# Loading half of one section of w_mod in four-partition transfers, one per iteration, in a decode block on one Trainium2 core

## The chip, the cores and the metric

The kernel runs on one core of a Trainium2 chip. The metric is the device time of one launch in microseconds, as the median of several runs. A core has a matrix engine (TensorE, PE in the profile, with PEld for its weight loads), VectorE (DVE), ScalarE (ACT), GpSimd (POOL) and SyncE (SP), which here only issues transfers. Sixteen DMA engines move the data of all transfers between HBM and SBUF, which has 128 partitions.

## The reference

Four sequences, one new token each, go through one conditioned block: attention over a cache of 4096 positions with 32 heads, and a gated MLP. A modulation matrix w_mod (512 x 3072) turns the condition c into six sections of 512 columns: shift, scale and gate of the attention (sa, ca, ga) and of the MLP (sb, cb, gb).

```python
mod = (silu(c) @ w_mod).reshape(4, 6, 1, 512)
sa, ca, ga, sb, cb, gb = (mod[:, k] for k in range(6))
h = layernorm(x) * (1 + ca) + sa
q = (h @ wq)                                  # 32 heads of 128
p = softmax(q . k_cache * 128 ** -0.5)        # 4096 positions
x = x + ga * ((p @ v_cache) @ wo)
h = layernorm(x) * (1 + cb) + sb
z = gelu(h @ w_in)                            # 512 -> 2 x 896
g = w_sp * layernorm(z[896:]) + b_sp
x = x + gb * ((z[:896] * g) @ w_out)
```

Matrices and caches are bfloat16. The two caches have 134 MB each; everything else together has some 14 MB.

## The kernel before

The work is cut into NT = 32 tiles of 4 heads of one sequence: tile i has group g = i // 4 and sequence b = i % 4. A tile's K and its V are 4 MB each, 32 KB in every partition. Both have two buffers (`kt` and `vt`).

**Before the loop.** SyncE issues wq_sb, wm_sb (five of the six sections of w_mod, `wm[:, :, 0:5 * D]`, four rows of w_mod in each partition), K0, K1 and V0. ScalarE issues c_sb and x_sb, four partitions each. c is turned into columns by TensorE transposes (`rows_to_cols`, L184) and its silu is taken there on 128 x 16 elements (L225 to L234), which gives cT. `mod_cols` (L236) multiplies sections of wm_sb by cT, so that the result stands in columns. With the first two sections the kernel makes hT, and from that the queries qbc.

**The loop, L530.** The order on each engine is written out by hand (`manual_schedule`). In iteration i VectorE multiplies the two halves of K by the queries (`mult`, L288), TensorE adds up over the head dimension by products with the identity (`reduce_d`, L294), VectorE finishes the scores of tile i - 1 (`scores`), ScalarE takes the exponentials (L326), and TensorE multiplies V of tile i - 2 (`pv`, L366). After the second half of the reduction SyncE is told to load K of tile i + 2 (`load_k`), and after `pv` it loads V of tile i (`load_v`). SyncE has one queue and issues in program order; each K or V load waits until its buffer is free.

At i == 2 the next three sections of wm_sb (ga, sb, cb) are multiplied into `modT`, the pool `pre` that holds wq_sb and wm_sb is closed, and the pool `wts` takes its memory: wo_sb in four pieces and wo_last are loaded. At i == 5 one is added to the cb part of modT. At i == L - 1 = 30 come V31 in five pieces, win_sb, wout_sb, and the last section gb of w_mod into a V buffer (`wg_sb`, L602).

**The tail, from L604.** The last V pieces are multiplied as they land (`o_last`), the second layernorm gives hT2 (it needs the sb and cb parts of modT), `gate` (L684) multiplies it by win_sb, L707 multiplies by wout_sb, and L715 by the last section of w_mod. Then the row is written out.

Of the kernel before, what the change touches and what calls it, by code (L numbers as in the profile page):

```python
# [8 lines left out]
BF16 = mybir.dt.bfloat16  # L9
F32 = mybir.dt.float32  # L10
AF = mybir.ActivationFunctionType
ALU = mybir.AluOpType
# [12 lines left out]
def kernel(  # L25
# [16 lines left out]
    nc = tc.nc  # L42
    P = 128
    B, _, D = A_x.shape
    _, H, SK, DH = A_k_cache.shape
    F = B_w_in.shape[1]
    FH = F // 2
    DJ = D // P
# [10 lines left out]
    LN_EPS = 1e-5  # L59
    L = NT - 1  # L60
    BL = B - 1

    ctx.enter_context(tc.manual_schedule())

    consts = ctx.enter_context(tc.tile_pool(name="consts", bufs=1))
# [7 lines left out]
    def ps_sm(shape, dtype=F32):  # L73
        return psum.tile(shape, dtype, name="sm", bufs=3)
# [6 lines left out]
    pre = pre_cm.__enter__()  # L81
    c_sb = pre.tile([B, D], BF16, name="c_sb")
# [4 lines left out]

    wq_sb = pre.tile([P, DJ, H * DH], BF16, name="wq_sb")
    nc.sync.dma_start(out=wq_sb, in_=A_wq.rearrange("(p j) n -> p j n", p=P))
    wm_sb = pre.tile([P, DJ, 5 * D], BF16, name="wm_sb")  # L90
    wm = w_mod.rearrange("(p j) n -> p j n", p=P)
    nc.sync.dma_start(out=wm_sb, in_=wm[:, :, 0:5 * D])

    def kv_view(cache, i):
        g, b = divmod(i, B)
# [16 lines left out]
    def load_v(i):  # L112
# [8 lines left out]
    ident_bf = consts.tile([P, P], BF16, name="ident_bf")  # L121
    make_identity(nc, ident_bf)
    ident_f = consts.tile([P, P], F32, name="ident_f")
# [19 lines left out]
        out=sel32, in_=ident_f.rearrange("p (q r) -> p r q", r=R), axis=AX.X, op=ALU.add  # L143
# [10 lines left out]
    for g in range(G):  # L154
        nc.vector.tensor_reduce(out=selg[:, g:g + 1], in_=idr[:, g], axis=AX.XY, op=ALU.add)
    nc.vector.tensor_reduce(
        out=sel4, in_=ident_f.rearrange("p (c b) -> p b c", b=B), axis=AX.X, op=ALU.add
# [3 lines left out]
        out=mask8, in_=ident_f.rearrange("p (h u) -> p h u", h=2 * HQ), axis=AX.X, op=ALU.add  # L161
# [3 lines left out]
    x1w = consts.tile([P, DJ, R], F32, name="x1w")  # L165
    nc.gpsimd.memset(x1w, 0.0)
    cT = consts.tile([P, DJ, B], BF16, name="cT")

    consts.tile([P, 512], mybir.dt.uint8, name="gap")
    wk.tile([P, 32], mybir.dt.uint8, name="gap", bufs=1)  # L170
    pbds, opss = [], []
    for k in range(3):
        t = consts.tile([P, NJ, HQ], BF16, name=f"pbd{k}")
        nc.gpsimd.memset(t, 0.0)
        pbds.append(t)
    for k in range(2):
        t = psum.tile([P, G, DH], F32, name=f"ops{k}", bufs=1)
# [3 lines left out]
    def bc(ap, n):  # L181
        return ap[:, None, :].to_broadcast([P, n, ap.shape[-1]])

    def rows_to_cols(src):  # L184
        t = ps_sm([P, DJ, B], BF16)
        for j in range(DJ):
            nc.tensor.transpose(t[:, j, :], src[0:B, j:D:DJ], ident_bf[0:B, 0:B])
        return t

    def across(rhs, mat):  # L190
# [13 lines left out]
    def normed(pool, src, name, then=None, last=None):  # L204
# [16 lines left out]
        rsqrt(rs, v, 1.0, eps)  # L221
        return xc, rs

    cps = rows_to_cols(c_sb)
    cx = pre.tile([P, DJ, B], F32, name="cx")  # L225
    nc.vector.tensor_copy(out=cx, in_=cps)
    sg = pre.tile([P, DJ, B], F32, name="sg")
    nc.vector.tensor_scalar(
        out=sg, in0=cx, scalar1=-60.0, scalar2=-1.0, op0=ALU.max, op1=ALU.mult
    )  # L230
    nc.scalar.activation(out=sg, in_=sg, func=AF.Exp)
    nc.vector.tensor_scalar_add(out=sg, in0=sg, scalar1=1.0)
    nc.vector.reciprocal(out=sg, in_=sg)
    nc.vector.tensor_tensor(out=cT, in0=cx, in1=sg, op=ALU.mult)  # L234

    def mod_cols(s0, n, dst):  # L236

        for m in range(n):
            s, j = divmod(m, DJ)
            c0 = (s0 + s) * D + j  # L240
            for k in range(DJ):
                nc.tensor.matmul(  # L242
                    dst[:, m, :], lhsT=wm_sb[:, k, c0:c0 + (P - 1) * DJ + 1:DJ], rhs=cT[:, k, :],
                    start=(k == 0), stop=(k == DJ - 1),
                )
# [11 lines left out]
        out=hs, in0=modA[:, DJ:2 * DJ, :], scalar=1.0, in1=xn, op0=ALU.add, op1=ALU.mult  # L257
# [83 lines left out]
    def whole(i):  # L341

        g, b = divmod(i, B)
        return slice(b, b + 1) if g == NQ - 1 else slice(0, B) if b == BL else None

# [86 lines left out]
    for n in set(SETS):  # L432
        picks[n] = consts.tile([P, n, P], BF16, name=f"pick{n}")
        for a in range(n):
            u = P // n
            nc.vector.tensor_copy(
                out=picks[n][:, :, a * u:(a + 1) * u],
                in_=ident_bf.rearrange("p (u r) -> p r u", r=n),
# [79 lines left out]
    modT = consts.tile([P, 3 * DJ, B], F32, name="modT")  # L518
# [6 lines left out]
    def add_up():  # L525
        while adds:
            o_add(*adds.pop(0))

    QPLAN = {0: (1, 2), 1: (3, 4, 5), 2: (6, 7)}
    for i in range(NT):  # L530
        more = list(QPLAN.get(i, ()))
        mult(i, 0)
        if i >= 1:
            scores(i - 1)
        if i >= 2:
            norm_b(i - 2)
        add_up()
        rows_up()
        dealt()
        if i >= 3:  # L540
            o_pick(i - 3)
        reduce_d(i, 0)
        if i >= 3:
            o_cols(i - 3)
        if more:
            queries(more.pop(0))
        mult(i, 1)
        if i >= 1:
            norm_r(i - 1)
        if i >= 3:  # L550
            o_scale(i - 3)
        sum8(i, 0)
        reduce_d(i, 1)
        load_k(i + 2)
        if i >= 1:
            norm_a(i - 1)
        project()
        if i - 3 in ends:
            deal(ends[i - 3])
        while more:  # L560
            queries(more.pop(0))
        if i >= 2:
            pv(i - 2)
        if i == 0:
            load_v(1)
        elif 2 <= i < L:
            load_v(i)
        if i == 2:
            nc.scalar.dma_start(out=sp_t[:, 0:1], in_=B_w_sp[0:1, 0:1])
            nc.scalar.dma_start(out=sp_t[:, 1:2], in_=B_b_sp.rearrange("(a b) -> a b", b=1))  # L570
            mps = ps_sm([P, 3 * DJ, B])
            mod_cols(2, 3 * DJ, mps)
            nc.vector.tensor_copy(out=modT, in_=mps)
            pre_cm.__exit__(None, None, None)
            wts = tl = ctx.enter_context(tc.tile_pool(name="wts", bufs=1))
            wo_sb = wts.tile([P, H - HQ, D], BF16, name="wo_sb")
            wo_last = wts.tile([P, HQ, D], BF16, name="wo_last")
            hl = (H - HQ) * DH
            h0 = 0
            for n in SETS:  # L580
                nc.sync.dma_start(
                    out=wo_sb[:, h0:h0 + n, :],
                    in_=A_wo[h0 * DH:(h0 + n) * DH].rearrange("(p r) n -> p r n", p=P),
                )
                h0 += n
            nc.sync.dma_start(out=wo_last, in_=A_wo[hl:H * DH].rearrange("(q p) n -> p q n", p=P))
        if i == 5:
            sps = ps_sm([P, 2])
            nc.tensor.matmul(sps, lhsT=ones_b, rhs=sp_t, start=True, stop=True)
            nc.vector.tensor_copy(out=spf, in_=sps)  # L590
            nc.vector.tensor_copy(out=g8[:, 1, :], in_=spf[:, 0:1].to_broadcast([P, B]))
            cbT = modT[:, 2 * DJ:3 * DJ, :]
            nc.vector.tensor_scalar_add(out=cbT, in0=cbT, scalar1=1.0)
        if i == L - 1:
            load_v(L)
            win_sb = wts.tile([P, DJ, F], BF16, name="win_sb")
            nc.sync.dma_start(out=win_sb, in_=B_w_in.rearrange("(p j) n -> p j n", p=P))
            wout_sb = wts.tile([P, NH, D], BF16, name="wout_sb")
            nc.sync.dma_start(out=wout_sb, in_=B_w_out.rearrange("(j p) n -> p j n", p=P))
            wg_sb = kvp.tile([P, NJ, DH], BF16, name="vt", bufs=2)  # L600
            wg_sb = wg_sb.rearrange("p n d -> p (n d)")[:, 0:DJ * D].rearrange("p (k n) -> p k n", k=DJ)
            nc.sync.dma_start(out=wg_sb, in_=wm[:, :, 5 * D:])  # L602
# [17 lines left out]
    o_scale(L - 1)  # L620
    adds.append((o_proj(0, BL), 0, BL))
    add_up()
# [6 lines left out]
    def sums():  # L629
# [21 lines left out]
        out=nv2, in0=mq2[:, 0:1], scalar=mq2[:, 0:1], in1=mq2[:, 1:2],  # L651
        op0=ALU.mult, op1=ALU.subtract,
# [6 lines left out]
        out=hl, in0=xs, scalar=mq2[:, 0:1], in1=cbT[:, :, BL], op0=ALU.subtract, op1=ALU.mult  # L659
    )  # L660
    nc.vector.scalar_tensor_tensor(
        out=hT2[:, :, BL], in0=hl, scalar=rsl, in1=sbT[:, :, BL], op0=ALU.mult, op1=ALU.add
# [4 lines left out]
        out=x1m, in0=x1[:, :, :, None].to_broadcast([P, DJ, B, HQ]),  # L667
        in1=mask4[:, None, None, :].to_broadcast([P, DJ, B, HQ]), op=ALU.mult,
    )
    x1r = ps_sm([B * DJ, P])  # L670
    for k in range(DJ):
        nc.tensor.matmul(
            x1r[:, k:P:DJ], lhsT=x1m[:, k].rearrange("p b j -> p (b j)"), rhs=sel32,
            start=True, stop=True,
# [4 lines left out]
    def gate(h):  # L679
# [21 lines left out]
        out=zz.rearrange("p f g b -> p g b f"), in0=z1[:, None].to_broadcast([P, 2, B, NH]),  # L701
        in1=st3[:, 0:2], op=ALU.mult,
    )
    y = ps_q()[:, 0:DJ * 2 * B].rearrange("p (j g b) -> p j g b", j=DJ, g=2)
    for j in range(DJ):
        for f in range(NH):
            nc.tensor.matmul(  # L707
                y[:, j], lhsT=wout_sb[:, f, j * P:(j + 1) * P], rhs=zz[:, f],
                start=(f == 0), stop=(f == NH - 1),
# [3 lines left out]
    for j in range(DJ):  # L713
        for k in range(DJ):
            nc.tensor.matmul(  # L715
                gb[:, j, :], lhsT=wg_sb[:, k, j * P:(j + 1) * P], rhs=cT[:, k, :],
                start=(k == 0), stop=(k == DJ - 1),
# [3 lines left out]
        out=mq3, in_=ps3.rearrange("p (g b f) -> p g b f", g=2, b=B), axis=AX.X, op=ALU.add  # L721
# [4 lines left out]
        out=rs3, in0=mq3[:, 1], scalar=LN_EPS, in1=rs3, op0=ALU.add, op1=ALU.subtract  # L726
# [3 lines left out]
        out=g8[:, 0, :], in0=mq3[:, 0, :], scalar=-1.0, in1=g8[:, 1, :], op0=ALU.mult, op1=ALU.mult  # L730
# [5 lines left out]
        out=t3[:, 2], in0=yb[:, 0], scalar1=spf[:, 1:2], scalar2=None, op0=ALU.mult  # L736
    )
    nc.vector.tensor_tensor(
        out=g8, in0=g8, in1=rs3[:, None, :].to_broadcast([P, 2, B]), op=ALU.mult
    )  # L740
    nc.vector.tensor_tensor(
        out=t3[:, 0:2], in0=g8[:, :, :, None].to_broadcast([P, 2, B, DJ]), in1=yb, op=ALU.mult
# [3 lines left out]
        out=tt, in_=t3.rearrange("p g b j -> p b j g"), axis=AX.X, op=ALU.add  # L746
# [37 lines left out]
```

## Time and profile before

| what | value |
|---|---|
| time, median of 3 runs | 667.55 us (667.23 to 667.95) |
| span of the profiled execution, first to last instruction | 665.8 us |
| PE, DVE, ACT busy | 60%, 63%, 13% of the span |
| DMA | 283.15 MB, 425 GB/s, SyncE's queue 98.9% of 16 engines' span |
| K and V loads (4096 KB), issue to landing, median | 23.0 and 30.7 us |
| mean granted TensorE clock | 0.828 |

The time of the profiled execution itself is not listed apart from its span; the median of the runs is 1.75 us above that span. The profile's page gives the busy time of each engine, the span in 40 equal slices with a digit for the busy tenths, the DMA queues with packets, megabytes and their share of the DMA engines' time, the chain of waits that ended last, and the transfers with the time from their issue to landing. In the timeline a row has start and duration in us, engine and line, the tiles, and in brackets how long the engine had been idle and what ended that. A q behind an engine's name is its instruction queue, where transfers are issued.

### The profile page before, as it was taken

The numbers are of one execution on the slowest core, as the hardware profiler recorded it, in microseconds if no ns is written. First come the engines' busy times: TensorE is split into PE (matmuls) and PEld (weight loads), VectorE is DVE, ScalarE is ACT, GpSimd is POOL, SyncE is SP. The second block draws the span as 40 slices with busy tenths as digits, with TensorE's granted clock in tenths as the row PEclk, the third lists the DMA queues.
The fourth block names the chain that finished last, engine by engine and source line by source line (L and its number), as shares of the span: only waits on it lengthen the run. The fifth ranks groups of instructions, "written<-read, shape, count | busy, mean of one in ns | idle before, by whom it ended". The sixth has DMA issues, their size and how long they took to land.

```text
span 665.8 us, 6509 instructions
## 1 busy us (share of the span) xinstructions
PE 399.3 (60%) x2674; PEld 175.4 (26%) x2674; DVE 419.5 (63%) x589; ACT 85.0 (13%) x278; POOL 3.8 (1%) x17
## 2 busy tenths in 40 slices
PE   1195795556556746754665467566555468666675
PEld 0132331222222312222222222222222223322245
DVE  3485592776565777655567756657765566776833
ACT  1021120111011111101111110111111011111112
POOL 1000000000000000000000000000000000000000
PEclk9998987777898778789877778787777897887975
DMA  8999999999999999999999999999999999999996
GB/s 363 452 419 433 431 417 435 436 437 422 439 432 438 422 439 433 436 423 436 435 431 426 438 435 432 426 436 437 431 426 437 435 429 432 433 436 421 438 419 234
DMA packets 13377, 283.15 MB, mean 425 GB/s; under 512 B 1308, under 2 KB 3236, under 8 KB 4132
## 3 DMA queue, kind: packets, MB, share of 16 engines
q1 hardware_dynamic: 13328, 282.73, 98.9%
q8 instruction: 21, 0.34, 0.2%
q14 instruction: 8, 0.07, 0.0%
q10 hardware_dynamic: 20, 0.01, 0.0%
HBM read 282.73 MB, written 0.00 MB: 425 GB/s over the span
## 4 chain that ended last, share of the span: by engine, by line
DMA 56%; DVE 28%; PE 13%; issue 1%; SPq 1%; ACT 0%; DVEq 0%
DMA kt<-in_A_k_cache_dram 52%; DVE kt L288 21%; PE red L294 11%; DMA win_sb<-in_B_w_in_dram 5%; DVE osb L378 2%; DVE S L303 1%; DVE mrow L312 1%; DVE osb L374 1%; PE ops L366 1%; SPq L104 1%; DVE mt L316 1%; DVE nM L318 0%; PE qps L274 0%; DVE mb L314 0%; DVE nM L319 0%
## 5 line engine op out<-in xcount | busy, mean ns | idle before, releaser
L294 PE MATMUL red<-kt,ident_bf 128*128 128x512 bf16 x1024 | 301.5, 461 | 236.4 <-DVE kt L288 236.4
L288 DVE TENSOR_TENSOR kt<-kt,qbc 128x8192 bf16<-128x8192 bf16 x64 | 282.8, 4420 | 185.2 <-DMA kt<-in_A_k_cache_dram 184.2
L294 PEld LDWEIGHTS <-ident_bf 128*128 128x128 bf16 x1024 | 118.9, 116 | 411.5 <-issue 285.8
L326 ACT ACTIVATE pbd<-S,nM 32x128 bf16<-32x128 f32 x128 | 73.8, 577 | 505.3 <-DVE nM L319 463.2
L366 PE MATMUL ops<-vt,pbd 128*16 128x512 bf16 x992 | 62.6, 388 | 1.4 <-DMA vt<-in_A_v_cache_dram 1.4
L303 DVE TENSOR_REDUCE S<-red 128x64 f32<-128x512 f32 x64 | 43.8, 684 | 5.8 <-PE red L294 5.8
L378 DVE SCALAR_TENSOR_TENSOR osb<-ops,selg,osb 128x128 f32<-128x128 f32 x93 | 32.6, 351 | 3.3
L326 ACT ACTIVATION_READ_ACCUMULATOR pbd<-S,nM 32x1 f32 x128 | 32.0, 250 | 0.0
L366 PEld LDWEIGHTS <-pbd 128*16 128x16 bf16 x992 | 23.2, 90 | 30.7 <-issue 8.5
L386 PEld LDWEIGHTS sm<-sel,osb 128*128 128x128 f32 x62 | 11.7, 194 | 7.4 <-issue 2.2
L374 DVE TENSOR_SCALAR osb<-ops,selg 128x128 f32<-128x128 f32 x31 | 10.1, 325 | 5.3 <-PE ops L366 5.3
L386 PE MATMUL sm<-sel,osb 128*128 128x4 f32 x62 | 9.2, 219 | 2.1 <-DVE osb L378 2.0
L278 ACT CAST qbc<-qps 128x512 bf16<-128x512 f32 x8 | 4.7, 585 | 45.3 <-PE qps L274 45.3
L274 PE MATMUL qps<-wq_sb,hTb 128*32 128x512 bf16 x128 | 9.2, 412 | 1.6 <-DVE hTb L262 0.9
L312 DVE TENSOR_REDUCE mrow<-S 128x1 f32<-128x128 f32 x32 | 9.2, 286 | 1.1
L242 PE MATMUL sm<-cT,wm_sb 128*128 128x4 bf16 x80 | 3.0, 173 | 8.3 <-DMA wm_sb<-in_w_mod_dram 8.3
L316 DVE STREAM_TRANSPOSE mt<-mb 128x32 f32<-128x32 f32 x32 | 6.8, 212 | 1.1
L337 DVE TENSOR_SCALAR rsb<-mask,rs 128x4 f32<-128x4 f32 x32 | 7.2, 224 | 0.4 <-ACT pbd L326 0.4
L318 DVE TENSOR_REDUCE nM<-mt 128x1 f32<-128x32 f32 x32 | 6.0, 186 | 1.1
L314 DVE COPY mb<-mrow 128x32 f32<-128x32 f32 x32 | 5.8, 181 | 1.1
L491 PE MATMUL sm<-wo_sb,od 128*4 128x512 bf16 x24 | 5.7, 379 | 0.0
L319 DVE TENSOR_SCALAR nM<-nM 128x1 f32<-128x1 f32 x32 | 4.9, 153 | 1.1
(136 smaller groups left out, 88.8 us busy)
## 6 DMA issues: line engine op xcount, KB each, us to landing
kt<-in_A_k_cache_dram SPq DMA_DIRECT2D x31, 4096.0 KB, 23.0
vt<-in_A_v_cache_dram SPq DMA_DIRECT2D x31, 4096.0 KB, 30.7
wq_sb<-in_A_wq_dram SPq DMA_DIRECT2D x1, 4096.0 KB, 12.3
kt<-in_A_k_cache_dram SPq DMA_DIRECT2D x2, 2048.0 KB, 16.7
wo_sb<-in_A_wo_dram SPq DMA_DIRECT2D x3, 1024.0 KB, 22.9
kt<-in_A_v_cache_dram SPq DMA_DIRECT2D x3, 1024.0 KB, 25.5
wm_sb<-in_w_mod_dram SPq DMA_DIRECT2D x1, 2560.0 KB
win_sb<-in_B_w_in_dram SPq DMA_DIRECT2D x1, 1792.0 KB
```

Of the source, the lines that this page charges most:

```text
L274: nc.tensor.matmul(qp[R * q:R * (q + 1)], lhsT=hTb[:, k, b, :], rhs=wq_v[:, k, gs, q, :], start=(k == 0), stop=(k == DJ - 1), tile_positio ...
L288: nc.vector.tensor_tensor(out=kt, in0=kt, in1=bc(qbc[:, g, b, :], KC), op=ALU.mult)
L294: nc.tensor.matmul(red, lhsT=ident_bf, rhs=kt[:, :, m * RD:(m + 1) * RD], start=(m == 0), stop=(m == DH // RD - 1),)
L303: nc.vector.tensor_reduce(out=st[i, "S"][:, kc * KC:(kc + 1) * KC], in_=st.pop((i, "red", kc)), axis=AX.X, op=ALU.add,)
L312: nc.vector.tensor_reduce(out=mrow, in_=S, axis=AX.X, op=ALU.max)
L316: nc.vector.transpose(mt, mb)
L326: nc.scalar.activation(out=pbd[r, :, q], in_=S[r, :], func=AF.Exp, bias=nM[r, :], scale=att_scale, accum_out=rs[r, :],)
L337: nc.vector.tensor_scalar(out=st[g, "rsb"][:, b, :], in0=mask4, scalar1=st.pop((i, "rs")), scalar2=None, op0=ALU.mult)
L366: nc.tensor.matmul(opss[i % 2][g:g + G * HQ], lhsT=pbds[i % 3][:, n, :], rhs=vts[i][:, n, :], start=(m < 4), stop=(m >= NJ // G - 4), tile ...
L374: nc.vector.tensor_scalar(out=osb, in0=ops[:, 0, :], scalar1=selg[:, 0:1], scalar2=None, op0=ALU.mult)
L378: nc.vector.scalar_tensor_tensor(out=osb, in0=ops[:, g, :], scalar=selg[:, g:g + 1], in1=osb, op0=ALU.mult, op1=ALU.add,)
L386: nc.tensor.matmul(op, lhsT=st.pop((i, "osb")), rhs=sel4, start=True, stop=True)
```

## The change

wm_sb holds four sections instead of five. The fifth, cb, is loaded later, into the memory that win_sb takes at the end (a tile `win` that both use). Its second 256 rows go to `w2`, 128 partitions with two rows each, in one transfer at i == 2, behind wo_last. Its first 256 rows go to `w4`, 32 partitions with eight rows each, in eight transfers of four partitions (i - 3, i + 5, i + 13, i + 21), one in each of the iterations 3 to 10, behind that iteration's V load. A transfer has 32 KB, eight rows of 1 KB in each of its four partitions.

At i == 14 the section is multiplied in rows: eight products over 32 partitions and two over 128, with 512 columns each, into a 4 x 512 result; one is added, and four small products turn it into columns for modT. For this the silu of c is now taken in rows (4 x 512 elements), and turned into columns three times: cT as before, cT4 for w4 and cT2 for w2.

```diff
+    P4 = 32
+    K4 = 8
+    D4 = P4 * K4
+    D2 = D - D4
+    K2 = D2 // P
...
-    wm_sb = pre.tile([P, DJ, 5 * D], BF16, name="wm_sb")
+    wm_sb = pre.tile([P, DJ, 4 * D], BF16, name="wm_sb")
     wm = w_mod.rearrange("(p j) n -> p j n", p=P)
-    nc.sync.dma_start(out=wm_sb, in_=wm[:, :, 0:5 * D])
+    nc.sync.dma_start(out=wm_sb, in_=wm[:, :, 0:4 * D])
...
-    def rows_to_cols(src):
-        t = ps_sm([P, DJ, B], BF16)
-        for j in range(DJ):
-            nc.tensor.transpose(t[:, j, :], src[0:B, j:D:DJ], ident_bf[0:B, 0:B])
+    def rows_to_cols(src, d0=0, d1=D, n=DJ):
+        t = ps_sm([(d1 - d0) // n, n, B], BF16)
+        for j in range(n):
+            nc.tensor.transpose(t[:, j, :], src[0:B, d0 + j:d1:n], ident_bf[0:B, 0:B])
         return t
...
-    cps = rows_to_cols(c_sb)
-    cx = pre.tile([P, DJ, B], F32, name="cx")
-    nc.vector.tensor_copy(out=cx, in_=cps)
-    sg = pre.tile([P, DJ, B], F32, name="sg")
+    sg = pre.tile([B, D], F32, name="sg")
     nc.vector.tensor_scalar(
-        out=sg, in0=cx, scalar1=-60.0, scalar2=-1.0, op0=ALU.max, op1=ALU.mult
+        out=sg, in0=c_sb, scalar1=-60.0, scalar2=-1.0, op0=ALU.max, op1=ALU.mult
     )
     nc.scalar.activation(out=sg, in_=sg, func=AF.Exp)
     nc.vector.tensor_scalar_add(out=sg, in0=sg, scalar1=1.0)
     nc.vector.reciprocal(out=sg, in_=sg)
-    nc.vector.tensor_tensor(out=cT, in0=cx, in1=sg, op=ALU.mult)
+    cs = pre.tile([B, D], BF16, name="cs")
+    nc.vector.tensor_tensor(out=cs, in0=c_sb, in1=sg, op=ALU.mult)
+    nc.vector.tensor_copy(out=cT, in_=rows_to_cols(cs))
+    nc.vector.tensor_copy(out=cT4, in_=rows_to_cols(cs, 0, D4, K4))
+    nc.vector.tensor_copy(out=cT2, in_=rows_to_cols(cs, D4, D, K2))
...
         if i == 2:
...
-            mps = ps_sm([P, 3 * DJ, B])
-            mod_cols(2, 3 * DJ, mps)
-            nc.vector.tensor_copy(out=modT, in_=mps)
+            mps = ps_sm([P, 2 * DJ, B])
+            mod_cols(2, 2 * DJ, mps)
+            nc.vector.tensor_copy(out=modT[:, 0:2 * DJ], in_=mps)
...
             nc.sync.dma_start(out=wo_last, in_=A_wo[hl:H * DH].rearrange("(q p) n -> p q n", p=P))
+            cw = wts.tile([P, DJ * F], BF16, name="win")
+            w4 = cw[0:P4, 0:K4 * D].rearrange("p (k n) -> p k n", k=K4)
+            w2 = cw[:, K4 * D:(K4 + K2) * D].rearrange("p (k n) -> p k n", k=K2)
+            cbR = cw[0:B, (K4 + K2) * D:(K4 + K2 + 2) * D].bitcast(F32)
+            w4v = w_mod[0:D4, 4 * D:5 * D].rearrange("(e s k) n -> s e k n", e=4, k=K4)
+            nc.sync.dma_start(
+                out=w2, in_=w_mod[D4:D, 4 * D:5 * D].rearrange("(p k) n -> p k n", p=P)
+            )
+        if 3 <= i < 3 + P4 // 4:
+            nc.sync.dma_start(out=w4[i - 3:P4:P4 // 4], in_=w4v[i - 3])
...
+        if i == 14:
+            cp = ps_sm([B, D])
+            for k in range(K4):
+                nc.tensor.matmul(cp, lhsT=cT4[:, k, :], rhs=w4[:, k, :], start=(k == 0), stop=False)
+            for k in range(K2):
+                nc.tensor.matmul(cp, lhsT=cT2[:, k, :], rhs=w2[:, k, :], start=False, stop=(k == K2 - 1))
+            nc.vector.tensor_scalar_add(out=cbR, in0=cp, scalar1=1.0)
+            cp = ps_sm([P, DJ, B])
+            for j in range(DJ):
+                nc.tensor.matmul(
+                    cp[:, j, :], lhsT=cbR[:, j:D:DJ], rhs=ident_f[0:B, 0:B], start=True, stop=True
+                )
             cbT = modT[:, 2 * DJ:3 * DJ, :]
-            nc.vector.tensor_scalar_add(out=cbT, in0=cbT, scalar1=1.0)
+            nc.vector.tensor_copy(out=cbT, in_=cp)
```

Nothing else of the computation changes, and the same bytes are read from HBM in all.

More of the change, by code (lines that the diff above doesn't have):

```diff
@@ L167 @@
     cT = consts.tile([P, DJ, B], BF16, name="cT")
-    consts.tile([P, 512], mybir.dt.uint8, name="gap")
+    cT4 = consts.tile([P4, K4, B], BF16, name="cT4")
+    cT2 = consts.tile([P, K2, B], BF16, name="cT2")
+    consts.tile([P, 416], mybir.dt.uint8, name="gap")
     wk.tile([P, 32], mybir.dt.uint8, name="gap", bufs=1)
@@ L591 @@
             nc.vector.tensor_copy(out=g8[:, 1, :], in_=spf[:, 0:1].to_broadcast([P, B]))
+        if i == 14:
[10 more added lines that the diff above has]
+                )
             cbT = modT[:, 2 * DJ:3 * DJ, :]
-            nc.vector.tensor_scalar_add(out=cbT, in0=cbT, scalar1=1.0)
+            nc.vector.tensor_copy(out=cbT, in_=cp)
         if i == L - 1:
             load_v(L)
-            win_sb = wts.tile([P, DJ, F], BF16, name="win_sb")
+            win_sb = wts.tile([P, DJ * F], BF16, name="win").rearrange("p (k n) -> p k n", k=DJ)
             nc.sync.dma_start(out=win_sb, in_=B_w_in.rearrange("(p j) n -> p j n", p=P))
```

## The prediction

> **What bounds the kernel now.** I read the page's slices first, then its DMA queues, its chain of waits, and last the timeline of the tail and the single DMA packets that the trace holds behind the totals of part 3.
>
> ```profile
> span 665.8 us, 6509 instructions
> DMA  8999999999999999999999999999999999999996
> GB/s 363 452 419 433 431 417 435 436 437 422 439 432 438 422 439 433 436 423 436 435 431 426 438 435 432 426 436 437 431 426 437 435 429 432 433 436 421 438 419 234
> q1 hardware_dynamic: 13328, 282.73, 98.9%
> q8 instruction: 21, 0.34, 0.2%
> q14 instruction: 8, 0.07, 0.0%
> ```
>
> Read the DMA rows first: from the second slice to the last but one the 16 DMA engines have no free tenth, and q1 (SyncE's transfers) holds 98.9% of their time. No compute engine is above 63%. So this is a stream of 282.73 MB, and an edit is worth what it does to the engine that finishes its share last. Rows q8 and q14 are instruction fetches; they matter below.
>
> ```profile
> DMA kt<-in_A_k_cache_dram 52%; DVE kt L288 21%; PE red L294 11%; DMA win_sb<-in_B_w_in_dram 5%; DVE osb L378 2%; DVE S L303 1%; DVE mrow L312 1%; DVE osb L374 1%; PE ops L366 1%; SPq L104 1%; DVE mt L316 1%; DVE nM L318 0%; PE qps L274 0%; DVE mb L314 0%; DVE nM L319 0%
> ```
>
> The multiplications in this chain are those that release a K buffer. They do not starve the stream: a K load is issued a median 23.0 us before it lands, and its own 4 MB take 9.7 us. K16, issued at 308.48, gets its first packet on the fastest engine near 319.3, 10.8 us later. The end of the chain and the tail behind it:
>
> ```profile
> 625.92 31.81 DMA win_sb<-in_B_w_in_dram
> ...
> 656.88 0.23 DVE L661 SCALAR_TENSOR_TENSOR hT<-hl,rsl,modT 128x4 bf16<-128x4 f32 x1 [0.37 <-ACT rsl L202]
> 657.78 1.65 PE L684 MATMUL red<-hT,win_sb 128*128 128x4 bf16 x56 [0.78 <-DMA win_sb<-in_B_w_in_dram]
> ...
> 660.06 0.89 PEld L707 LDWEIGHTS <-wout_sb 128*128 128x128 bf16 x28 [0.29 <-DMA wout_sb<-in_B_w_out_dram]
> ...
> 661.38 0.58 PE L715 MATMUL sm<-cT,vt 128*128 128x4 bf16 x16 [0.34 <-DMA vt<-in_w_mod_dram]
> ```
>
> hT2 is ready at 657.11, yet the gate product waits until win_sb lands at 657.73; wout_sb and the last section of w_mod are awaited in the same way. A DMA lands when its last engine is through. So the end follows the slowest engine.
>
> **Which engine that is.** In the packet records one engine's packets follow each other without a gap (a 32 KB packet every 1.210 us), so 16 chains can be followed from start to end. Only instruction fetches push a chain for good: a 16 KB packet of q8 delays the one it hits by 1.41 to 1.42 us, an 8 KB packet of q14 by 0.54 or 0.83 to 0.85 us. The q8 hits go round eight engines; q14 hits always return to the same few. No stall gives the others' lead back: the semaphores of one transfer come within 0.65 us of each other for wq_sb, 1.9 at V0, 2.6 by 164 us, 4.0 by 445 us, and 4.6 for win_sb. On the slowest chain win_sb's last packet ends at 657.31.
>
> Now the engines that a transfer of four rows uses. c_sb and x_sb are such transfers: each left four data packets of 1 KB and four semaphore packets in q10, where every 128-partition transfer leaves 16 semaphores. The packets of x_sb (6.21, 6.31, 6.35, 6.59 us) each push one chain by 39 ns, which names the four. Two of them are never hit by a fetch and run 4.6 us ahead of the slowest at win_sb. A third has two q14 hits and is 3.3 us ahead. The fourth takes a q14 hit at 42.8, 200.1, 355.8, 516.4 and 655.0 us: its win_sb ends at 656.88, only 0.43 us before the slowest.
>
> **The change, part by part, per DMA engine.**
> - wm_sb loses a fifth: each engine still has 32 packets, of 4 KB instead of 5 KB. From semaphore to semaphore the 5 KB packets take 192.9 ns each and 4 KB ones (wo_sb's last piece) 155.2: 32 x 37.7 = -1.21 us.
> - w2: 256 packets of 1 KB, 16 for each engine. wo_last's 32 took 1.361 us with a 6 ns semaphore, 42.4 ns each: 16 x 42.4 + 6 = +0.68 us. Those two give -0.52 us on every engine.
> - w4: eight transfers of 4 partitions x 8 rows of 1 KB. By the rows of c_sb and x_sb, 4 engines get 8 packets each: 8 x (8 x 42.4 + 6) = +2.76 us on these four and nothing on twelve. If SyncE's queue spread the rows over all 16, it would be 64 x 42.4 ns / 4 = +0.69 us on each. I take the first end, since those are the only transfers with four rows in the trace; they are on ScalarE's queue.
>
> So twelve engines end 0.52 us earlier, four end 2.24 us later. For three of the four that is inside their lead. The fourth ends win_sb at 656.88 + 2.24 = 659.12, against 657.31 for the slowest now: +1.81 us. The same engine is 0.43 us from the slowest at wout_sb (659.26 against 659.68) and at the last w_mod section (660.62 against 661.05), so all three waits of the tail move by +1.81. The last piece of V31 moves less (651.78 + 2.24 against 652.73: +1.29), so hT2 would be ready near 658.4, still ahead of win_sb at 659.54. The twelve can't matter: 656.79 at win_sb.
>
> [...]
>
> Everything else I cost at nothing, by its cover:
> - SyncE: nine more issues of about 0.35 us. After wo_last it is idle from 80.97 to 94.21 and after each V issue for over 10 us (V14 310.33, K17 328.31). No K or V issue comes later.
> - The silu of c in rows: four VectorE passes over 4x512. From accR's rows (0.67 us) three cost 2.0 us; the reciprocal goes by 0.176 us for 4 columns and 0.25 for 16, so 6.2 ns per column, 3.4 us for 512. With Exp at about 0.6, fourteen transposes and three copies, the x path that took 8.2 to 11.9 ends near 15.8. modA needs it near 19.3 (wm_sb lands at about 18.0, and 1.2 us of matmuls follow). Cover gone, the cost is what exceeds 3.5 us, and K0's landing near 27.7 hides 3 us or more beyond that.
> - Iteration 2: 16 products of 0.036 us fewer ahead of the copy to modT; SyncE waits on them only for wo_sb, issued at 78.47 with its first packet near 96.0.
> - Iteration 14: ten products of 0.38 us, one 0.67 us addition, four small fp32 products and a copy stand ahead of mult(15,0) on VectorE, until about 315.5 instead of 312.64. Queued behind are scores(14), the rest of iteration 15 and K17's issue, 328.31 to about 331.2. K17's packets are first wanted near 338.4: 7 us are left. If that cover were gone, up to 2.9 us.
> - The early pinch: K4 is issued near 74.3, just as the first engines finish K3 (76.3), and eight engines restart late there. Both sides of it move 1.21 us earlier, so it stays as it is. The fourth engine is late enough there (77.54) to lose nothing.
>
> Sum: span 665.8 + 1.8 = 667.6. The median of the runs, 667.55, lies 1.75 above this span, and I keep that: **669.35 us**. A measurement here can tell about 0.2% from no change, 1.34 us, so the threshold is 668.89.
>
> **Rivals.**
> 1. The four-row transfers are spread (over 16 engines, or starting from another engine each time). Then every engine gets -0.52 + 0.69 = +0.17: 667.7. For it: no row shows SyncE's queue with few rows. Against it: c_sb and x_sb stay on four engines, and both sp_t loads, of one row, are on the first of them. [...]
> 2. The other side, faster: the slow member has a lead after all. It decides at a lead of 2.76 us over the four: with more, nothing but -0.52 is left, 667.0, and not below 0.2%. For it: three of four have that lead here, and the runs spread by 0.7 us. Against: the fourth's lead is 0.43, made of five fetches that its engine takes each time. For a gain beyond 0.2% the pinch at K4 would have to vanish too.
> 3. Something costs more: the silu in rows past its cover, or 1 KB packets on few engines slower than 42.4 ns (at twice that, +2.7 us more): 670 to 672.5.
>
> **How the numbers follow.** The forecast has 0.70, with its own range 668.8 to 669.9 (the runs' spread of 0.7 and the start offsets of the chains, up to 0.65). Rival 1 has 0.11, rival 2 0.09, rival 3 0.10. The range leaves out most of rivals 2 and 3: 667.6 to 670.3. Slower: nine tenths of the forecast and rival 3, 0.73. Faster: 0.04, from rival 2 with the pinch gone. Same: the remaining 0.23.
>
> **What would show it.** Per step: wm_sb landing 1.2 us earlier and K0's first multiplication near 27.8; each w4 transfer as four semaphores; a spread among the engines of win_sb's landing of about 7.0 us instead of 4.6 (4.21 + 2.76, since one of the three foremost chains is not among the four); the gate product at L684's counterpart waiting for win_sb until near 659.6; wout_sb waited for in the same way; K loads never awaited for lack of issue. It would be wrong if w4 left 16 semaphores, if the late member were another engine, or if VectorE ran late before K0.

## The result, and the profile after

The changed kernel takes 671.11 us (median of 5 runs, 670.66 to 672.85) against 667.91 us of the kernel before (5 runs beside it, 667.23 to 668.68): a ratio of 1.0055, with a 95% interval of 1.0044 to 1.0066, or +2.9 to +4.4 us (+3.7 by the ratio; the medians differ by 3.2). The forecast of +1.8 us had the direction and lies outside that interval; 671.11 is also 0.8 us above its range. The profiled execution after is the slowest of its five (672.85 us, 1.85 us around its span), which has a reason that comes up below.

The page after, at the rows that were read before:

```profile
span 671.0 us, 6546 instructions
DMA  8999999999999999999999999999999999999994
GB/s 364 450 435 427 402 413 442 428 418 439 434 423 422 436 431 432 429 434 429 432 431 436 435 432 431 432 433 432 433 436 430 431 433 434 434 431 427 438 418 158
q1 hardware_dynamic: 13888, 282.73, 98.4%
q8 instruction: 21, 0.34, 0.2%
q14 instruction: 8, 0.07, 0.0%
```

It is still a stream without a free tenth, with the same bytes in q1 and 560 packets more. The fifth and the last slice stand out: 402 instead of 431 GB/s at about 67 to 84 us, and 158 instead of 234 at the end, where one engine works alone (it ends win_sb 4.0 us behind the next).

The chain of waits and then the timeline of the tail (start and duration in us; brackets: idle before, and what ended it):

```profile
629.70 33.27 DMA win<-in_B_w_in_dram
662.97 0.05 issue
663.02 1.67 PE red L714 x56
```

```profile
661.58 0.23 DVE L691 SCALAR_TENSOR_TENSOR hT<-hl,rsl,modT 128x4 bf16<-128x4 f32 x1 [0.37 <-ACT rsl L209]
663.02 1.65 PE L714 MATMUL red<-hT,win 128*128 128x4 bf16 x56 [1.33 <-DMA win<-in_B_w_in_dram]
665.26 0.94 PEld L737 LDWEIGHTS <-wout_sb 128*128 128x128 bf16 x28 [0.24 <-DMA wout_sb<-in_B_w_out_dram]
666.61 0.59 PE L745 MATMUL sm<-cT,vt 128*128 128x4 bf16 x16 [0.33 <-DMA vt<-in_w_mod_dram]
```

hT2 is ready at 661.81 and the gate product waits until 663.02 for win, as predicted for this place; wout_sb and the last section of w_mod are awaited behind it. It waits for one engine. In the packet records the engine that takes the q14 fetches (here at 42.7, 192.1, 350.6, 507.5, 659.0 us) ends its part of win_sb at 662.53; the next latest chain ends at 658.48. That is the late member that the prediction named, and it is later than forecast.

**What the packet records show beside that.** Exactly four engines carry w4, eight packets of 46 ns each (one every 42.3 ns), as the sum had it. But around every one of the w4 transfers a cluster of K and V packets is slow: a 32 KB packet takes 1.213 us elsewhere, and near 167 us at least one on each of the 16 engines takes 1.31 to 1.51, six of them exactly 1.371. Between 145 and 269 us seven such clusters hold 1.5 to 2.9 us of excess each, summed over 16 engines; the first, at 125.8, has 0.3. The kernel before has none after 95 us, apart from fetches. 

**The early pinch.** K3 ends 1.24 us earlier than before (mean over the engines), but from the end of K3 to that of K4 this execution takes 11.05 us instead of 10.09. K4 is issued at 73.37 (before 74.02), only 0.65 us earlier, and TensorE's reductions ahead of it were slower than before:

```profile
32.15 6.21 PE L302 MATMUL red<-kt,ident_bf 128*128 128x512 bf16 x16 [10.15 <-DVE kt L296]
62.32 6.48 PE L302 MATMUL red<-kt,ident_bf 128*128 128x512 bf16 x16 [5.38 <-DVE kt L296]
```

Before, the same two took 5.54 and 5.78 us. So there were two candidates for the missing 1.4 us: the pinch, and the w4 transfers' effect on their neighbours.

### The profile page after: what moved, and what is told of

Same layout as the page of the kernel before. It is cut to its first block, busy times and chain, and to the rows that moved or that the text cites. A ratio compares the mean times of both kernels' runs of the same rounds, so it can differ in the third digit from the quotient of the medians.

```text
span 671.0 us, 6546 instructions
## 1 busy us (share of the span) xinstructions
PE 402.0 (60%) x2686; PEld 177.3 (26%) x2686; DVE 424.6 (63%) x592; ACT 85.7 (13%) x278; POOL 3.8 (1%) x17
## 4 chain that ended last, share of the span: by engine, by line
DMA 57%; DVE 28%; PE 12%; issue 1%; SPq 1%; ACT 0%; DVEq 0%
DMA kt<-in_A_k_cache_dram 52%; DVE kt L296 21%; PE red L302 11%; DMA win<-in_B_w_in_dram 5%; DVE osb L386 2%; DVE S L311 1%; DVE mrow L320 1%; DVE osb L382 1%; PE ops L374 1%; DVE mt L324 1%; DVE nM L326 0%; PE qps L282 0%; DVE mb L322 0%; SPq L109 0%; DVE nM L327 0%
## 5 line engine op out<-in xcount | busy, mean ns | idle before, releaser
L286 ACT CAST qbc<-qps 128x512 bf16<-128x512 f32 x8 | 4.7, 587 | 42.4 <-PE qps L282 42.4
```

## The experiments

All ratios are to the kernel before, run on the same chip beside it (medians 667.49 to 667.61 us). A difference in us stands for its ratio, unless two medians are named.

**1. The changed kernel without w4.** Left out are the eight transfers and their eight products.

```diff
-        if 3 <= i < 3 + P4 // 4:
-            nc.sync.dma_start(out=w4[i - 3:P4:P4 // 4], in_=w4v[i - 3])
...
-            for k in range(K4):
-                nc.tensor.matmul(cp, lhsT=cT4[:, k, :], rhs=w4[:, k, :], start=(k == 0), stop=False)
```

> The changed kernel without the eight four-partition transfers and without their eight products (the first 256 rows of the section are left out of the computation); wm_sb, w2, the silu in rows and the order stay. Three theories on the change's +3.2 us over the kernel before. A, what was predicted: only the data of the eight transfers on the late engine counts (+2.76, of which 0.43 is cover, less 0.52). B: each four-partition transfer also slows the packets of all sixteen engines around it, by 0.15 to 0.3 us, 1.2 to 2 us in all. C: the shorter wm_sb lets the queue run dry at K4 for longer, about 1 us. Against the kernel before, A expects -0.5 us and B -0.5 us, with no slowed packets after 110 us; C expects +0.5 us.

Measured: 667.07 us, ratio 0.9994 (0.9985 to 1.0003), that is -0.4 us. The terms wm_sb and w2 alone make -0.52. The clusters are gone. So the silu in rows, the smaller wm_sb, w2 and the row form of the section cost nothing that shows; all of the loss comes with w4, by its transfers or its products.

**2. The kernel before with the eight transfers added.** They go to memory that nobody reads.

```diff
+            cw = wts.tile([P, DJ * F], BF16, name="win")
+            w4 = cw[0:32, 0:8 * D].rearrange("p (k n) -> p k n", k=8)
+            w4v = w_mod[0:256, 4 * D:5 * D].rearrange("(e s k) n -> s e k n", e=4, k=8)
+        if 3 <= i < 11:
+            nc.sync.dma_start(out=w4[i - 3:32:8], in_=w4v[i - 3])
...
```

> The kernel before with the eight four-partition transfers added, in the same place and form, into memory that nobody reads; wm_sb keeps its five sections, so the early part up to K4 is that of before and 256 KB more are loaded in all. The late engine's 4.21 us behind the front plus 2.76, against 4.64 of the slowest: A expects +2.3 us over the kernel before. B expects +3.5 to +4.3 and the clusters of slowed 32 KB packets around each of the eight transfers. C expects +2.3 and no clusters.

Measured: 671.72 us, ratio 1.0063 (1.0050 to 1.0075), +4.2 us. Data alone give 2.76 less the late engine's distance of 0.43, +2.33. Seven of the eight transfers have a cluster, of 0.8 to 2.8 us; the first has 0.12. Apart from `win`, which w4 and win_sb share, nothing else of the change is in this kernel, so the transfers themselves bring the excess.

**3. One transfer of 32 partitions instead of eight of four.**

```diff
-            w4v = w_mod[0:D4, 4 * D:5 * D].rearrange("(e s k) n -> s e k n", e=4, k=K4)
+            w4v = w_mod[0:D4, 4 * D:5 * D].rearrange("(p k) n -> p k n", k=K4)
-        if 3 <= i < 3 + P4 // 4:
-            nc.sync.dma_start(out=w4[i - 3:P4:P4 // 4], in_=w4v[i - 3])
+        if i == 3:
+            nc.sync.dma_start(out=w4, in_=w4v)
```

> The changed kernel with w4 loaded by one transfer of 32 partitions at iteration 3 instead of eight of four; bytes, rows and products are the same. The transfer goes over all sixteen engines, 16 packets of 1 KB each, 0.68 us. A expects -0.52 + 0.69 = +0.2 us against the kernel before. B expects +0.2 to +0.5, since only one transfer is left to slow others. C expects +1.2, the dry stretch at K4 being that of the changed kernel.

Measured: 669.57 us, ratio 1.0036 (1.0021 to 1.0051), +2.4 us (the medians differ by 2.0; one of the six runs took 672.62): a miss for every theory then held, and the run that changed the view. The data are now spread over all 16 engines, 0.69 us on each. Yet in one cluster from 124.3 to 130.0 us, 44 packets of 32 KB lose 22.9 us, 1.43 for each engine; the longest takes 2.4 us, and many 1 KB packets take 100 to 170 ns. The slices show it as one dent:

```profile
GB/s 362 453 425 421 438 421 439 387 432 423 436 435 434 433 428 434 437 434 427 434 434 434 429 430 437 436 431 430 429 438 434 433 425 432 440 433 423 434 422 227
```

In the eighth slice (117 to 134 us) it moves 387 GB/s. So a transfer that leaves no engine out is dear too. The 1 KB packets of w2, which go over all 16 engines to 128 partitions, all take 46 ns (run 7). What is different here is the 32 partitions, and hence the question of where each engine writes.

**4 and 5. The pinch.** In the changed kernel and in the one before, the queries of one group are made behind the second reduction of iteration 2 instead of between the two, so that K4 can be issued earlier.

```diff
-        if more:
+        if more and i != 2:
             queries(more.pop(0))
```

> The changed kernel with queries(6) in iteration 2 moved behind the second half of the reduction, so that K4 can be issued about 1 us earlier (near 72.4 instead of 73.4). A and B expect the time of the changed kernel, +3.2 us over the kernel before (B: at most 0.3 less). C expects +2.2 or less, and no gap in the DMA chains at the start of K4.

> The kernel before with queries(6) in iteration 2 behind the second half of the reduction, so that K4 is issued near 73.0 instead of 74.0 us, ahead of the point at which the first engines finish K3 (76.3). If the late start of K4 costs the kernel before the 0.3 to 0.4 us by which all engines fall back there, it gains 0.3 to 0.4 us; if what comes later takes the lead away, it stays as it is.

Measured: 671.01 us, ratio 1.0052 (1.0039 to 1.0066), for the changed kernel, which is as slow as without the edit (671.11); K4 is issued at 72.05 there, K3 to K4 takes 9.72 us, nothing is lost, and the clusters are all there. The kernel before stays at 0.9997 (0.9988 to 1.0005). The pinch is not what the typical run pays.

It does go with the spread between runs. Ten profiles with the order of before, by the first reduction of tile 2 and the time from K3's to K4's mean end: 5.09 and 9.79 us (run 10), 5.12 and 9.78 (8), 5.13 and 9.69 (3), 5.56 and 9.75 (1), 5.60 and 9.74 (6), 5.78 and 10.09 (before), 6.32 and 10.87 (7), 6.36 and 11.17 (9), 6.42 and 10.58 (2), 6.48 and 11.05 (after). K's 4 MB alone take 9.7. The row of run 6 that stands against the slow one above:

```profile
62.26 5.60 PE L302 MATMUL red<-kt,ident_bf 128*128 128x512 bf16 x16 [6.27 <-DVE kt L296]
```

What makes it slow is the granted clock. The next two rows are the stretch from 66 to 68 us, first of the changed kernel and then of run 6; the last three numbers are the granted clock, the DMA share and GB/s:

```profile
66.00:68.00 2.00, 2.00 (x6) 0.73 (x5) 2.00 (x1) 0.52 (x2) 0.00 (x0) 0.50 0.80 336
66.00:68.00 2.00, 2.00 (x12) 0.76 (x14) 2.00 (x1) 0.46 (x2) 0.00 (x0) 0.92 0.73 303
```

In each of the ten profiles the clock stands at 0.5 for 6.83 us around here, and that stretch ends at another point: at 68.16 us in the changed kernel, 66.32 in run 6, 65.40 in run 3. The reduction takes the 3.6 us of a reduction at full clock plus half of the time that it shares with the stretch, in all ten to within 0.05 us. What places the stretch is open. Where it covers most of the reduction, K4 ends up to 1.4 us later (11.17 against 9.75). The four profiled executions with 10.58 us or more took 0.6 to 1.7 us longer than the medians of their kernels, those with 9.8 or less at most as long as theirs.

**6. Four partitions next to each other.** Transfer s goes to partitions 4s to 4s + 3 instead of s, s + 8, s + 16, s + 24.

```diff
-            w4v = w_mod[0:D4, 4 * D:5 * D].rearrange("(e s k) n -> s e k n", e=4, k=K4)
+            w4v = w_mod[0:D4, 4 * D:5 * D].rearrange("(s e k) n -> s e k n", e=4, k=K4)
-            nc.sync.dma_start(out=w4[i - 3:P4:P4 // 4], in_=w4v[i - 3])
+            nc.sync.dma_start(out=w4[4 * (i - 3):4 * (i - 2)], in_=w4v[i - 3])
```

> The changed kernel with w4's transfer number s going to the four partitions 4s to 4s + 3 instead of s, s + 8, s + 16, s + 24; the same rows per partition, bytes, engines and products. [...] Theory Q: any transfer that leaves engines out costs all engines some 0.15 us, wherever it lands: +3.2 us, as the changed kernel.

Measured: 671.70 us, ratio 1.0060 (1.0047 to 1.0072), +4.0 us. The clusters look different: at 164.9 us it is the packet behind w4 on each of the four carrying engines that is slow (1.29, 1.55, 1.60, 1.92 us), and few others are. The time is that of the changed kernel within the intervals (+3.7): with adjacent targets the price stays, on other packets.

**7. Eight partitions, four apart.** Four transfers of eight partitions, s, s + 4, ..., s + 28. From here on P is the author's guess that the target partitions decide whether a transfer costs more than its data; the choice of targets four apart was part of that guess.

```diff
-            w4v = w_mod[0:D4, 4 * D:5 * D].rearrange("(e s k) n -> s e k n", e=4, k=K4)
+            w4v = w_mod[0:D4, 4 * D:5 * D].rearrange("(e s k) n -> s e k n", e=8, k=K4)
-        if 3 <= i < 3 + P4 // 4:
-            nc.sync.dma_start(out=w4[i - 3:P4:P4 // 4], in_=w4v[i - 3])
+        if 3 <= i < 3 + P4 // 8:
+            nc.sync.dma_start(out=w4[i - 3:P4:P4 // 8], in_=w4v[i - 3])
```

> The changed kernel with w4 loaded by four transfers of eight partitions (s, s + 4, ..., s + 28, in iterations 3 to 6), over eight engines; partitions, rows, bytes and products are the same. [...] P: only the data counts, 4 x 0.345 = 1.38 on eight engines, the late one at 4.21 - 0.52 + 1.38 = 5.07 against 4.64 before: +0.4 us over the kernel before, no clusters of slowed packets. Q: four transfers instead of eight, +0.4 and 4 x 0.15 to 0.25: +1.0 to +1.4, with four clusters.

Measured: 668.11 us, ratio 1.0009 (1.0000 to 1.0018), +0.6 us; no cluster at any of the four transfers, every 1 KB packet at 46 ns. This computes all that the change computes. The data on the late engine are 4 x (8 x 42.4 + 6 ns) = 1.38 us, so that the sum of the prediction gives 1.38 - 0.52 - 0.43 = +0.43.

**8. Run 2 with targets four apart.** The same eight transfers, four engines, 32 KB, unread; only the target partitions differ: s, s + 4, s + 8, s + 12 for s = 0 to 3, and the same 32 partitions further on. "Own paths" in labels and expectations, and "paths kept apart", stand for these targets.

```diff
...
+            w4 = cw[0:48, 0:8 * D].rearrange("p (k n) -> p k n", k=8)
+            w4v = w_mod[0:256, 4 * D:5 * D].rearrange("(e s k) n -> s e k n", e=4, k=8)
+        if 3 <= i < 11:
+            p0 = i - 3 if i < 7 else 32 + i - 7
+            nc.sync.dma_start(out=w4[p0:p0 // 32 * 32 + 16:4], in_=w4v[i - 3])
...
```

> [...] P: the data alone, +2.3 us over the kernel before and no clusters of slowed packets. Q: +4.2 us and the clusters of e2_extra_w4.

Measured: 670.00 us, ratio 1.0035 (1.0021 to 1.0048), +2.3 us: the number of the data alone. No cluster, all packets of 1 KB at 46 ns. The two chains of waits, first run 2 and then run 8:

```profile
629.82 32.62 DMA win<-in_B_w_in_dram
662.48 1.67 PE red L689 x56
```

```profile
627.37 32.73 DMA win<-in_B_w_in_dram
660.14 1.67 PE red L690 x56
```

The gate product starts 2.34 us earlier, and the medians differ by 1.7. (The profiled execution of run 2 had a slow reduction at the pinch, that of run 8 a fast one, which goes the way of the rest.) The same moment in the packet records, durations in ns of successive 32 KB packets, on the four carrying engines and then on three of the others (w4 stands for the eight packets of 1 KB):

```
changed kernel, 164.4 to 169.8 us      run 8, 163.5 to 167.6 us
1213 1213 w4 1384 1213                 1213 w4 1213 1213 1213
1213 1380 w4 1336 1213                 1213 w4 1213 1213
1213 w4 1227 1335 1219                 1213 w4 1213 1213
1213 w4 1281 1309 1213                 w4 1213 1213 1213
1213 1213 1371 1213 1213               1213 1213 1213 1213
1213 1214 1367 1213 1213               1213 1213 1213 1213
1213 1213 1360 1213 1213               1213 1213 1213 1213
```

**9. The changed kernel with targets four apart.** Run 8's targets in the changed kernel; the eight products with w4 are left out.

> [...] Left out are the eight products with w4. Theory P (the excess over the data comes from writing into another engine's partitions): the number of the prediction's sum, +1.8 us over before (669.3 if before is at 667.5), all packets of 1 KB at 46 ns, no cluster of slowed 32 KB packets between 110 and 280 us, the late engine's win_sb 2.0 to 2.5 us behind where the next one ends. Theory Q (something else in the changed kernel is missing from the sum, the pinch at K4, the products or the row form of the silu): +3 us or more with the paths kept apart.

Measured: 669.66 us, ratio 1.0032 (1.0019 to 1.0044), +2.1 us (1.3 to 2.9). This is the prediction's own number, +1.8, inside its interval, with all packets of 1 KB at 46 ns and no cluster. The late engine ends win_sb 2.8 us behind the next one, a little more than the 2.0 to 2.5 expected. Its five runs, 669.19, 669.45, 669.66, 670.55 and 671.06, fall into two groups a good 1 us apart; the profiled one, 671.06, has a K3 to K4 of 11.17 us.

**10. Targets 36 apart.** Run 2's form with seven rows of 1 KB in each partition, to partitions s, s + 36, s + 72, s + 108; nobody reads them.

```diff
...
+            w4v = w_mod[0:224, 4 * D:5 * D].rearrange("(e s k) n -> s e k n", e=4, k=7)
+        if 3 <= i < 11:
+            o = (i - 3) // 4 * 7
+            p0 = (i - 3) % 4
+            nc.sync.dma_start(out=w4[p0:p0 + 109:36, o:o + 7], in_=w4v[i - 3])
...
```

> [...] By data alone on the late engine (8 x (7 x 42.4 + 6 ns) = 2.42 us instead of 2.76) and the 2.5 us that the same transfers on own paths cost: +2.1. [...]

Measured: 670.08 us, ratio 1.0035 (1.0021 to 1.0049), +2.3 us (1.4 to 3.3). With the whole of what run 2 costs above run 8 (4.2 less 2.3, 1.9 us) on top of the 2.1 it would be +4.0, which the interval excludes; +2.1 and half of that on top, some +3.0, can't be told apart. The packets say more: from the second transfer on the clusters hold 0.5 to 0.7 us, in 5 to 11 packets; the first holds 0.15, in three. That is less than in run 2 (0.8 to 2.8 us from the second on). In the one at 164.4 us five packets take over 1.23 us, on four engines: two of the carrying engines (1.25 and 1.26 us behind w4), and two that carry no w4 (1.41 and 1.24; 1.44). The other two carriers have none. The records don't name engines; which packets are one engine's is read off the times.

## Why the prediction was partly right

Its terms, against what was measured:

- wm_sb -1.21: landed 1.2 us earlier, and K0's first multiplication began at 27.67 (forecast near 27.8). Right. Run 1, -0.4 us for wm_sb and w2 together, agrees with -0.52.
- Silu in rows, at nothing: the reciprocal took 3.34 us (estimate 3.4), the normalised x was ready at 14.91 (15.8), and wm_sb was waited for. Right.
- Iteration 14, at nothing: the cover held, but on less than stated. mult(15, 0) started at 320.50, not 315.5, and K17 was issued at 336.15, not 331.2; the first engine reached K17 at 339.65, so the margin was 3.5 us, not 7. The products were not dearer than forecast: mult(15, 0) came 5.3 us behind the end of `pv` (315.24), and the forecast's 315.5 lies 5.2 us behind that end before (310.28). The whole iteration ran 5.0 us later in this execution, because a load lands with its latest engine: K14's semaphores came from 291.24 to 297.33 us, where before they came from 289.91 to 292.49. The prediction gave the late engine its 2.24 us at the end alone; here they also hold up every K, while the foremost engine wants K17 only 1.3 us later than before. These are the multiplications of K14's first half, before and after:

```profile
292.81 4.43 DVE L288 TENSOR_TENSOR kt<-kt,qbc 128x8192 bf16<-128x8192 bf16 x1 [6.47 <-DMA kt<-in_A_k_cache_dram]
297.77 4.43 DVE L296 TENSOR_TENSOR kt<-kt,qbc 128x8192 bf16<-128x8192 bf16 x1 [6.49 <-DMA kt<-in_A_k_cache_dram]
```

- w4, four engines and the late one among them: right, by the packets and by the engine that ends last. Its data, 8 x (8 x 42.4 + 6 ns) = +2.76: right too. Run 8, which adds just that, came to +2.3 where 2.33 was due; run 9 shows the whole sum, +2.1 for +1.8.
- **The step that failed** is the price of w4, taken as its data and 6 ns for each transfer. Those 6 ns came from transfers over 128 partitions (before, wo_sb's 1 MB pieces follow each other at 2.453 us, which is eight 8 KB packets and 6 ns). With few partitions the price held where the targets are four apart (runs 7, 8, 9: +0.6, +2.3 and +2.1 us where the sum gives 0.43, 2.33 and 1.81). In the change, with targets eight apart, K and V packets are held up: +1.5 us (671.11 against 669.66 in run 9; 1.7 between runs 2 and 8), some 0.2 us for each of the eight transfers where the sum had 6 ns. The missing term is the time of the neighbouring 32 KB packets, not the transfer's own.
- The pinch, "stays as it is": wrong in some executions, by up to 1.4 us, since what decides is how much of tile 2's first reduction falls into the stretch at half clock (5.1 to 6.5 us). It widens the runs' spread (670.66 to 672.85) more than it moves the median: run 4, without it, is no faster.
- The third rival, 670 to 672.5, gives the right time for a wrong reason: 1 KB packets stayed at 46 ns. The spread at win_sb was 8.6 us where 7.0 was forecast.
- Two small readings were off and change nothing: K16's first packet is at 318.96, not near 319.3, so 10.5 us after its issue; and 64 x 42.4 ns / 4 is 0.68, not 0.69.

With targets four apart the transfers of 32 KB cost no more than their data as far as can be told (+2.3 for 2.33 in run 8). None of the 20 transfers with such targets (runs 7, 8, 9) left a cluster. Of the other 33 (runs 2, 3, 6, 10 and the changed kernel) 31 did, and the first of run 2 and of run 10 left three slow packets each (0.12 and 0.15 us). That the target partitions decide is shown by runs 2 and 8, which differ in nothing else (+4.2 and +2.3 us). By what means they decide was not shown: no record names an engine or the partitions that it writes.

Three things stay open. In the changed kernel near 167 us all 16 engines lose the same 150 ns or so at once, though only four carry w4; in run 6, with adjacent targets, it is the four carriers that lose. The medians of both come out within 0.6 us of each other all the same. And in each of these kernels the first of the eight transfers has the smallest cluster.

No version came out faster than the kernel before: even with a quarter megabyte left out (run 1) the gain can't be told from none. Of the versions that do what the change does, run 7 is the cheapest, at +0.6 us.

## What to carry to other kernels

In a stream that fills the DMA engines, price a small transfer by which engines carry it and how far the slowest of them is from the end, and look at what its target partitions do to the packets around it. The same 256 KB, in place of as much in wm_sb, cost +0.6 (run 7), +2.1 (run 9, without the products) and +3.7 us (the change) here, by stride and number of partitions. And when the sum rests on a row from another form of transfer, the neighbours' packets are where the difference will show.

## What the runs showed of the hardware

- A transfer of four partitions with 8 KB each slowed other transfers' packets where its targets were eight apart: in the changed kernel, from the second transfer on, 24 to 55 packets of 32 KB each time, from 1.213 us to at most 1.53. With targets four apart (runs 7, 8, 9): none.
- One transfer of 32 adjacent partitions, 256 KB, cost each of 16 engines 1.43 us in their 32 KB packets beyond its data (run 3).
- One and the same reduction early in the program takes 5.1 to 6.5 us from one kernel's profile to the next, by how much of it falls into a stretch of 6.83 us at a granted clock of 0.5. A load that is issued just in time behind it comes up to 1.4 us later by that.
